# Loading the first three x tiles and wq slices in column pieces over two DMA queues, with a shorter warm-up filler

## Chip, cores, metric

One core of one Trainium2 chip. The metric is the device time of one execution in microseconds (us), as the median of several executions. A ratio is the mean time of one kernel's fast runs over the mean of the other's in the same rounds, so it isn't quite the ratio of the medians that stand beside it; below 1 is faster. The intervals are 95% intervals.

## The reference, cut to what matters

The kernel mixes a linear-attention block and an MLP block over the same input `x` (2048 tokens, 640 columns, bf16). Only its beginning matters here: `x @ wqkv`, of which the first third gives the queries.

```python
def _A_ref(x, wqkv, wo):
    B, S, D = x.shape
    H = 32; Dh = D // H
    qkv = (lambda x, *d: x.transpose(*d))((x @ wqkv).reshape(B, S, 3, H, Dh), 2, 0, 3, 1, 4)
    q, k, v = qkv[0], qkv[1], qkv[2]
    phi = lambda t: jnp.where(t > 0, t + 1, jnp.exp(t)) + 1e-6
    ...
x = A_x
g = _sigmoid((x * gate_w).sum(-1, keepdims=True))
return g * a + (1 - g) * b      # a: attention block, b: MLP block
```

## The kernel before

`x` is held as 16 tiles of 128 tokens; `wq` (and `wk`, for the keys, which the profile calls wkg) as 5 slices of 128 rows. A whole tile or slice is 128 rows of 1280 B, 160 KB. A product of tile t and slice k needs tile t turned (columns to partitions) and slice k. The first loads are issued from two queues, SyncE ("sp") and ScalarE ("act"):

```python
load_x(0)                # all load_x on "sp"
load_wq(0, "act")
load_x(1)
load_wq(1, "act")
load_x(2)
load_wq(2, "act")
load_wq(3, "sp")
load_wq(4, "act")
load_wk(0, "sp")
...                      # wk 1 to 4, x tiles 3 and 4
x_turn(3)                # tiles from 3 on are turned by a DMA, issued from "sp"
...
for t0, t1 in ((5, 8), (8, NT)):
    dma_in(x_tok[:, t0:t1, :], ...)                  # 480 KB, then 1280 KB
    for t in range(4 if t0 == 5 else t0, t1):
        x_turn(t)
```

TensorE first runs fillers on a constant (to raise its clock and to pass the time), then turns tiles 0 to 2 itself (five 128-column transposes each, copied out of PSUM by VectorE) and takes up the products as slices arrive. A pair (t, k) is a matmul of 512 columns and one of 128; (t, None) is the turn of tile t.

```python
WARM = 3456              # six fillers of 512 columns, three of 128
addA(("warm",), 0.0, lambda: warmup(WARM, 0.834))
addA(("tx", 0), 0.28, lambda: t_x(0))
addA(("warm", 1), 0.0, lambda: warmup(WARM2, 0.42))
addA(("q", 2), 4.08, q_three)
def q_three():
    order = [(0, 0), (1, None), (0, 1), (1, 0), (1, 1), (2, None), (0, 2), (1, 2), (2, 0), (2, 1), (2, 2),
             (0, 3), (0, 4), (1, 3), (1, 4), (2, 3), (2, 4)]
    stream(order, wq, 128, lambda t, b: phi(b, pq_tok[:, t + 1, :]))
```

## Time and profile before

| | before |
|---|---|
| median of six runs | 260.03 us (259.23 to 260.79) |
| profiled execution, span | 257.8 us |
| TensorE busy | 98% |
| x tile 0 complete (issued 0.79) | 3.85 us |
| wq slice 1, slice 2 complete | 4.85, 6.46 us |
| first product with slice 1, with slice 2 (start of its weight load) | 5.05, 6.50 us |

"Complete" is the time at which the last of the 16 DMA engines that carry a transfer has reported. The prediction below shows the views themselves. The span is counted from the first instruction, so it is about 1.2 us shorter than the time of the execution.

### The profile page before, as it was taken

What the parts mean: (1) busy time and instruction counts of PE and PEld (TensorE: products, weight loads), DVE (VectorE), ACT (ScalarE), POOL (GpSimd) and SP (SyncE); (2) the same over time, 40 slices, a digit from 0 to 9 for tenths busy, and PEclk for the clock granted to TensorE, in tenths of its full rate; (3) what the DMA queues carried; (4) which work ended last, traced back from release to release, by engine and by line L of the source; (5) the groups of instructions that cost most, each with busy time, mean ns of one, the idle gap of its engine ahead of it and who ended that gap; (6) DMA issues with size and microseconds to landing.
All of it is one profiled execution on the core that took longest, in us unless ns stands there. A gap on an engine that the chain in (4) does not pass through costs nothing.

```text
span 257.8 us, 3932 instructions
## 1 busy us (share of the span) xinstructions
PE 253.0 (98%) x1485; PEld 126.4 (49%) x1512; DVE 144.2 (56%) x286; ACT 108.2 (42%) x221; POOL 90.4 (35%) x144
## 2 busy tenths in 40 slices
PE   8999999999999999999999999999999999999996
PEld 4555555544454544555444445444444744445554
DVE  2697888899964993679999600499600033200023
ACT  1497676651366858675853321001540100253000
POOL 5011499976952162658917000133100021300000
DMA  7766699646636699474646620114200022200011
GB/s 220 208 152 212 118 149 220 190 93 121 124 79 80 123 397 293 85 80 76 127 45 123 123 51 3 31 25 127 53 0 0 3 59 73 102 4 0 0 51 53
DMA packets 55891, 26.25 MB, mean 102 GB/s; under 512 B 47252, under 2 KB 54461, under 8 KB 55872
## 3 DMA queue, kind: packets, MB, share of 16 engines
q1 hardware_dynamic: 53696, 21.61, 38.5%
q0 software_dynamic: 1168, 3.28, 5.3%
q10 hardware_dynamic: 1008, 1.11, 1.2%
q8 instruction: 12, 0.20, 0.3%
q14 instruction: 7, 0.06, 0.1%
HBM read 12.04 MB, written 2.62 MB: 57 GB/s over the span
## 4 chain that ended last, share of the span: by engine, by line
PE 95%; DMA 2%; ACT 1%; issue 1%; DVE 0%; ACTq 0%
PE ps L604 51%; PE ps L1218 30%; PE ps L808 8%; DMA wq<-in_A_wqkv_dram 2%; PE ps L925 2%; PE ps L1253 1%; ACT hsT L660 1%; PE ps L1131 1%; PE ps L926 1%; DVE x_tok L643 0%; PE ps L1012 0%; PE ps L1041 0%; ACTq L285 0%; ACT junk L659 0%
## 5 line engine op out<-in xcount | busy, mean ns | idle before, releaser
L604 PE MATMUL ps<-xnT,w 128*128 128x512 bf16 x350 | 80.0, 379 | 0.5 <-issue 0.2
L643 DVE SCALAR_TENSOR_TENSOR x_tok<-ps,stg,abx 128x512 bf16<-128x512 f32 (+1 forms) x20 | 13.3, 670 | 80.6 <-PE ps L1218 58.6
L660 ACT ACTIVATE h2T<-ps 128x512 bf16<-128x512 f32 x52 | 30.5, 598 | 61.6 <-PE ps L604 61.5
L604 PEld LDWEIGHTS ps<-xnT,w 128*128 128x128 bf16 x360 | 34.5, 98 | 39.7 <-issue 0.5
L1218 PE MATMUL ps<-w,h2T 128*128 128x512 bf16 (+1 forms) x254 | 47.7, 346 | 0.3
L626 POOL TENSOR_SCALAR xn<-x_tok,st 128x640 bf16<-128x640 bf16 x32 | 35.2, 1107 | 25.7 <-DMA xnT<-xn 25.2
L626 POOL TENSOR_SCALAR abx<-x_tok,stg 128x640 f32<-128x640 bf16 x16 | 15.4, 970 | 70.8 <-DVE x_tok L643 70.8
L1218 PEld LDWEIGHTS ps<-w,h2T 128*128 128x128 bf16 x260 | 23.2, 98 | 24.5 <-issue 0.3
L660 ACT ACTIVATE Er<-ps 128x640 bf16<-128x640 f32 (+1 forms) x35 | 22.9, 660 | 14.9 <-PE ps L604 10.1
L659 ACT ACTIVATE junk<-x_tok 128x640 bf16<-128x640 bf16 x32 | 23.6, 737 | 2.8 <-DVE x_tok L641 2.5
L660 ACT ACTIVATE hsT<-ps 128x512 bf16<-128x512 f32 (+1 forms) x32 | 19.0, 594 | 11.3 <-PE ps L604 10.8
L604 PE MATMUL ps<-w,hsT 128*128 128x128 bf16 (+1 forms) x159 | 23.5, 298 | 0.2
L604 PE MATMUL ps<-wkg,xT 128*128 128x512 bf16 (+1 forms) x138 | 21.3, 298 | 0.1
L641 DVE SCALAR_TENSOR_TENSOR x_tok<-ps,x_tok 128x640 bf16<-128x640 f32 x16 | 13.1, 820 | 12.2 <-ACT junk L659 7.7
L1218 PE MATMUL ps<-M_sb,pqnT 128*128 128x512 bf16 (+1 forms) x98 | 19.6, 347 | 0.1
L604 PEld LDWEIGHTS ps<-w,hsT 128*128 128x128 bf16 x160 | 13.3, 98 | 12.3
L1160 DVE TENSOR_TENSOR pq_tok<-pq_tok,dnr 128x300 bf16<-128x300 bf16 (+1 forms) x48 | 18.5, 438 | 0.6
L808 PE MATMUL ps<-pk_tok,x_tok 128*128 128x512 bf16 x78 | 17.6, 379 | 0.1
L604 PEld LDWEIGHTS ps<-wkg,xT 128*128 128x128 bf16 x140 | 11.9, 97 | 11.2
L626 DVE TENSOR_SCALAR Er<-Er 128x640 bf16<-128x640 bf16 (+1 forms) x35 | 12.2, 348 | 8.0 <-ACT Er L660 7.4
L634 DVE TENSOR_TENSOR qprod<-qprod,pk_tok 128x640 f32<-128x640 f32 x13 | 16.3, 1252 | 0.4
L604 PE MATMUL ps<-wq,xT 128*128 128x512 bf16 (+1 forms) x69 | 16.2, 367 | 0.1
(89 smaller groups left out, 234.5 us busy)
## 6 DMA issues: line engine op xcount, KB each, us to landing
w<-in_B_w_dram SPq DMA_DIRECT2D x1, 2160.0 KB, 9.9
w<-in_B_w_dram SPq DMA_DIRECT2D x1, 2080.0 KB, 15.5
out_dram<-x_tok SPq DMA_DIRECT2D x3, 640.0 KB, 3.2
x_tok<-in_A_x_dram SPq DMA_DIRECT2D x1, 1280.0 KB, 6.4
w<-in_B_w_dram POOLq DMA_DIRECT2D x8, 160.0 KB, 4.6
x_tok<-in_A_x_dram SPq DMA_DIRECT2D x5, 160.0 KB, 3.9
wv<-in_A_wqkv_dram POOLq DMA_DIRECT2D x1, 800.0 KB, 5.6
wq<-in_A_wqkv_dram ACTq DMA_DIRECT2D x4, 160.0 KB, 4.2
```

Source lines behind the costliest of these rows:

```text
L604: ins = e.matmul(out_ap, l, r, start=(i == 0), stop=(i == n - 1))
L626: return engf(lambda e: e.tensor_scalar(out_ap, in_ap, s1, s2, op0, op1), rd, [out_ap], cost=cost)
L634: return engf(lambda e: e.tensor_tensor(out_ap, a, b_, op), [a, b_], [out_ap], cost=cost)
L641: return dve(lambda e: e.scalar_tensor_tensor(out_ap, in0, scalar, in1, op0, op1, accum_out=accum), rd, [out_ap, accum], cost=cost + 70.0)
L643: return dve(lambda e: e.scalar_tensor_tensor(out_ap, in0, scalar, in1, op0, op1), rd, [out_ap], cost=cost)
L659: return act(lambda e: e.activation(out_ap, in_ap, func, bias=bias, scale=scale, accum_out=accum), rd, wr, cost=cost)
L660: return act(lambda e: e.activation(out_ap, in_ap, func, bias=bias, scale=scale), rd, wr, cost=cost)
L808: ins = e.matmul(o, l, r, start=(t0 + q_ == 0), stop=(t0 + q_ == NT - 1))
L925: e.matmul(ps[:, b, 0:512], l, w[:, k, 0:512], start=(k == 0), stop=(k == KD - 1))
L926: return e.matmul(ps[:, b + 1, 0:n2], l, w[:, k, 512:512 + n2], start=(k == 0), stop=(k == KD - 1))
L1160: dve(lambda e, o=o, i0=i0, i1=i1: e.tensor_tensor(o, i0, i1, ALU.mult), [i0, dnr[:, 1, sd, :]], [o], cost=cost)
L1218: ins = e.matmul(o, l, r, start=first and i == 0, stop=last and i == len(prs) - 1, skip_group_check=True)
```

## The change

The intent is to have x tile 0 sooner by letting both queues carry it, and to start the real work earlier by as much: the filler loses one 512-column matmul. All six first transfers are cut, so twelve are issued.

```diff
-    load_x(0)
-    load_wq(0, "act")
-    load_x(1)
-    load_wq(1, "act")
-    load_x(2)
-    load_wq(2, "act")
+    for i in range(3):
+        for queue, n0, n1 in (("sp", 0, 256), ("act", 256, D)):
+            sch.dma(queue, x_tok[:, i, n0:n1], x2[128 * i:128 * (i + 1), n0:n1], "x%d%s" % (i, queue))
+        for queue, n0, n1 in (("sp", 256, D), ("act", 0, 256)):
+            sch.dma(queue, wq[:, i, n0:n1], A_wqkv[128 * i:128 * (i + 1), n0:n1], "wq%d" % i, group_total=2)
...
-    WARM = 3456
+    WARM = 2944
```

## The prediction

> **What bounds the kernel now.** I read the page first: engine shares, then the chain that ended last.
>
> ```profile
> PE 253.0 (98%) x1485; PEld 126.4 (49%) x1512; DVE 144.2 (56%) x286; ACT 108.2 (42%) x221; POOL 90.4 (35%) x144
> ...
> PE 95%; DMA 2%; ACT 1%; issue 1%; DVE 0%; ACTq 0%
> PE ps L604 51%; PE ps L1218 30%; PE ps L808 8%; DMA wq<-in_A_wqkv_dram 2%; PE ps L925 2%; PE ps L1253 1%; ACT hsT L660 1%; PE ps L1131 1%; PE ps L926 1%; DVE x_tok L643 0%; PE ps L1012 0%; PE ps L1041 0%; ACTq L285 0%; ACT junk L659 0%
> ```
>
> TensorE is busy 98% of the span and is 95% of the chain. The one other piece of size is the load of wq, 2% of 257.8 us or about 4.7 us: the start. Only that start is touched by the change, so I went there: the chain of waits in time order, then the waits of the first 14 us.
>
> ```profile
> 1.72 4.73 DMA wq<-in_A_wqkv_dram
> 6.50 0.39 PE ps L925
> ...
> PEld ps L615 <- DMA x_tok<-in_A_x_dram: 0.3, 1, 0.3
> PEld ps L925 <- issue: 0.3, 1, 0.3
> PEld ps L925 <- DMA wq<-in_A_wqkv_dram: 0.3, 1, 0.3
> ```
>
> The chain passes from the issue of wq slice 2 at 1.72 us through its landing to the matmul at 6.50 us. The columns of the waits are total, times, longest. So before 6.50 TensorE has three holes of 0.3 us each (until x tile 0 lands; until its turned copy is there, put down to "issue"; until wq slice 2 lands). After 6.50 no DMA wait is listed for it up to 14 us. What TensorE does in those first microseconds, from the timeline of that engine (start, duration, instruction):
>
> ```profile
> 0.83 2.93 PE L881 MATMUL ps<-const-bfloat16-1.0 128*128 128x512 bf16 x9 [0.83 <-PEq L1448]
> 3.90 0.45 PE L615 MATMUL ps<-ident,x_tok 128*128 128x128 bf16 x5
> ...
> 4.53 0.38 PE L925 MATMUL ps<-wq,xT 128*128 128x512 bf16 x1
> 4.75 0.22 PE L926 MATMUL ps<-wq,xT 128*128 128x128 bf16 x1
> 4.80 0.46 PE L615 MATMUL ps<-ident,x_tok 128*128 128x128 bf16 x5
> 5.10 0.38 PE L925 MATMUL ps<-wq,xT 128*128 128x512 bf16 x1
> ...
> 5.92 0.44 PE L615 MATMUL ps<-ident,x_tok 128*128 128x128 bf16 x5
> ...
> 6.50 0.39 PE L925 MATMUL ps<-wq,xT 128*128 128x512 bf16 x1
> ```
>
> The nine fillers (six of 512 columns, three of 128) end where x tile 0 arrives. How hard the load path works, from the table of one-microsecond stretches (the last two columns are the busy share of the 16 DMA engines and GB/s):
>
> ```profile
> 2.00:3.00 1.00, 1.00 (x4) 0.39 (x3) 0.00 (x0) 0.00 (x0) 0.92 (x6) 1.00 0.63 198
> 3.00:4.00 1.00, 0.86 (x7) 0.42 (x6) 0.00 (x0) 0.34 (x1) 0.84 (x4) 1.00 1.07 388
> 4.00:5.00 1.00, 0.87 (x12) 0.59 (x12) 0.65 (x2) 0.94 (x1) 0.72 (x5) 1.00 1.04 358
> 5.00:6.00 1.00, 1.00 (x13) 0.63 (x11) 0.71 (x3) 0.00 (x0) 0.00 (x0) 1.00 0.94 287
> 6.00:7.00 1.00, 0.86 (x12) 0.51 (x9) 0.57 (x3) 0.00 (x0) 0.00 (x0) 1.00 1.06 359
> ```
>
> From 3 us on the DMA engines are full. The start is bound by their bytes, not by when transfers are issued: wq slice 3 is issued at 2.18 and lands at 7.29, a backlog of several microseconds.
>
> **What the Trainium skill says.** "DMA: Bandwidth & Descriptors", section "Issuing engines are not separate DMA queues": transfers from different issuers run on the same 16 engines and interleave; using more issuers saves only sequencer time. The trace agrees: x tile 0 (one queue) and wq slice 0 (the other), both issued at 0.8, land at 3.85 and 4.02, so neither had the engines alone. The same page, section "Why small descriptors are slow (HBM only)", speaks of a fixed overhead per packet. The trace agrees: a packet of 256 B takes 18 ns, one of 1024 B 46 ns, one of 1280 B 55 ns, one of 3456 B 135 ns (medians of the packet records), a line of 8.7 ns plus 0.0365 ns per byte. "TensorE: Matmul & The Clock Gate", Part 1, says the array runs at half clock until a free-running window of about 3.4 us was busy. The trace agrees on the step: fillers of 512 columns start 427 ns apart, and between 3.45 and 3.54 us the 128-column ones tighten; after that pairs of 512 and 128 columns start 270 ns apart.
>
> **The change part by part.** Instruction order on TensorE, VectorE and GpSimd is unchanged except for one 512-column filler less and a split wait before the first transposes.
>
> Filler: minus 427 ns, so its last matmul starts at about 3.1 and the queue is free at about 3.2 instead of 3.6 us. Worth something only if x tile 0 is there sooner.
>
> x tile 0: both queues now carry it first. Its 64 KB on the first queue used to be the first 64 of 160 KB. From packet records binned by 0.2 us, that queue has moved 64 KB by about 2.65 and 160 KB by 3.21; the landing of the whole came 0.64 later, so the small piece lands near 3.3. The other queue starts at 2.22, has 96 KB by about 3.1, lands near 3.65. So x tile 0 is complete some 0.2 us earlier than 3.85; its first block, which alone gates the first matmul, 0.5 earlier.
>
> First matmul: it now waits for wq slice 0, in both queues behind the x pieces, near 4.15 (4.02 before plus packet overhead). Against 4.50 that is a gain of 0.3 us, at this point.
>
> Packet overhead: a row of 1280 B is 55 ns of an engine; 512 plus 768 B is 27.4 + 36.7 = 64.1 ns (estimates from the line above). Each engine moves 8 rows of each 160 KB transfer: 8 x 9 = 73 ns more, and 9 ns for one more semaphore write: 0.08 us per transfer, on engines that are full. By the sixth transfer that is 0.08 x 6 = 0.49 us, of which about 0.1 lies in the slow first stretch, where the engines wait anyway.
>
> wq slice 2: each queue carries the same 480 KB up to it as before, so it lands at 6.46 + 0.4 = 6.85 us if its slowest engine sets it as before, or about 6.5 if spreading evens that out (x tile 2 landed at 5.58, so the other queue was ahead). This is the **last wait of the start**, and it decides: after it TensorE runs without holes. The 0.3 gained at the first matmul is eaten at slices 1 and 2: I get 5.2 for the second slice's matmul (5.05 before) and 6.5 to 6.85 for the third's (6.50 before).
>
> Issue: 12 issues instead of 6, each about 0.45 us, 6 per queue: the last piece of slice 2 is issued at 3.15 us, not 1.72. Supply is 160 KB per 0.47 us, demand 160 KB per 0.53 us (8 x 64.1 + 18 ns), so issue stays just ahead of the engines. ScalarE's table load moves from 3.66 to about 5.1 and ends near 6.4, before the first exponential at 8.61: free.
>
> Later loads come 0.5 us later: wq slice 3 lands at 7.8 and wk slice 2 at 10.1 where the stream took them up at 7.87 and 10.05; with the stream itself 0.15 later that just fits, and costs 0.1 at most if it doesn't. The turned x tiles have over 0.7 us to spare (tile 4 lands at 15.49, is used at 16.3).
>
> Sum: the matmul stream after 6.5 us starts between 0.0 and 0.35 us later, 0.15 in the middle; against 260.07 that is plus 0.1%.
>
> **The rivals.**
> First, the intended gain: if the slow early packets (up to 0.67 us, before 2.4 us) overlap better over two queues, and the even split removes the slow tail of slice 2, the third wait shrinks: minus 0.3 us or a little more, 259.7. For: the three holes are 0.9 us together. Against: engines at 1.04 to 1.07 busy from 3 us.
> Second, the clock: with less filler and new holes from 3.2 on, the busy window may be missed and the next one ends some 3.4 us later. The first four pairs (270 ns more each) and the fifteen transposes (56 ns more each) then run at half speed: 1.9 us, less some 0.6 us of holes that they fill, so 1.3, 261.4. For: the old step came at 3.5, close to the cut. Against: about 2.4 of the first 3.5 us stay busy.
> Third, issue becomes the bound: pieces of 64 KB every 0.45 us leave the engines idle; slice 2 would land after 7, plus 0.5 us or more, 260.6.
>
> **Range and chances.** All paths lie within 0.6% of the time before, and its own three runs span 259.23 to 260.79, which is wider than the effect. I take plus 0.15, 260.2 us, and plus or minus 1.0 for the spread of runs and the clock: 259.2 to 261.2. Two per cent is 5.2 us, more than the whole start could give or take: chances 0.01 faster, 0.98 within, 0.01 slower.
>
> **What would show it.** Right: transposes of x tile 0 start before 3.7, the first matmul on wq near 4.2, the third slice's first matmul at 6.5 to 6.85 still released by the load of wq, and DMA packets up by some 860 (128 more rows and 16 more semaphore writes in each of six transfers). Rival one: that matmul at 6.2 or earlier. Rival two: 512-column matmuls 427 ns apart past 4 us. Rival three: DMA share clearly below 1 between 3 and 6 us. I am wrong if the time moves by over 1 us, or if a wait appears after 7 us that was not there.

## The result

The changed kernel takes 261.06 us (six runs, 260.5 to 261.72) against 260.03: ratio 1.004, interval 1.0015 to 1.0065. That is within 2%, but it is a real loss of about 1.0 us.

The page of the changed kernel: engine shares, the packet count, and the chain that ended last.

```profile
PE 255.4 (98%) x1511; PEld 126.6 (49%) x1511; DVE 144.5 (56%) x286; ACT 108.3 (42%) x221; POOL 90.0 (35%) x144
...
DMA packets 56755, 26.26 MB, mean 101 GB/s; under 512 B 47348, under 2 KB 55325, under 8 KB 56736
...
PE 92%; DMA 5%; SPq 2%; DVE 0%; issue 0%
```

The chain's DMA share went from 2 to 5%, and the issuing queue of SyncE, not there before, has 2%. Packets are up by 864. TensorE's timeline of the start (L615 is the turn, L924 the 512-column part of a product, L925 in the kernel before):

```profile
3.24 0.74 PE L615 MATMUL ps<-ident,x_tok 128*128 128x128 bf16 x5
...
4.12 0.45 PE L924 MATMUL ps<-wq,xT 128*128 128x512 bf16 x1
...
4.82 0.62 PE L615 MATMUL ps<-ident,x_tok 128*128 128x128 bf16 x5 [0.18 <-DMA x_tok<-in_A_x_dram]
6.06 0.39 PE L924 MATMUL ps<-wq,xT 128*128 128x512 bf16 x1 [0.62 <-DMA wq<-in_A_wqkv_dram]
...
7.03 0.44 PE L615 MATMUL ps<-ident,x_tok 128*128 128x128 bf16 x5
...
7.62 0.39 PE L924 MATMUL ps<-wq,xT 128*128 128x512 bf16 x1
```

The first turn comes 0.66 us earlier (3.90 before) and the first product 0.41 earlier (4.53). Then the gain is lost: the second turn is level (4.80), slice 1's first product 0.96 us later (5.10), slice 2's 1.12 later (6.50). The waits of the first 30 us, those of TensorE's weight load (total us, times, longest; L604 are the later products):

```profile
PEld ps L924 <- DMA wq<-in_A_wqkv_dram: 1.4, 3, 0.8
PEld ps L604 <- DMA xT<-x_tok: 1.1, 1, 1.1
PEld ps L615 <- DMA x_tok<-in_A_x_dram: 0.9, 2, 0.6
PEld ps L924 <- DMA wkg<-in_A_wqkv_dram: 0.5, 1, 0.5
```

Waits for wq grew from 0.3 to 1.4 us, those for x from 0.3 to 0.9, and two are new: for wk slice 2 (at 11.4 us) and for turned tile 4 (at 18.8). And the table of one-microsecond stretches (last two columns: share of the DMA engines, GB/s), to be held against the one in the prediction:

```profile
3.00:4.00 1.00, 1.00 (x10) 0.79 (x8) 0.23 (x1) 0.00 (x0) 0.84 (x4) 1.00 0.88 235
4.00:5.00 1.00, 0.77 (x4) 0.23 (x3) 0.42 (x1) 0.00 (x0) 0.71 (x5) 1.00 0.85 230
5.00:6.00 1.00, 0.44 (x5) 0.23 (x4) 0.71 (x3) 0.90 (x1) 0.00 (x0) 1.00 0.97 264
6.00:7.00 1.00, 0.94 (x6) 0.42 (x6) 0.00 (x0) 0.38 (x1) 0.00 (x0) 1.00 0.90 284
```

The loads moved at 230 to 284 GB/s, not 287 to 388, and the engines were no longer full. What completed when (last engine's report, us):

| | before | changed, first trace | changed, second trace |
|---|---|---|---|
| x tile 0 | 3.85 | 3.25 | 3.26 |
| wq slice 0 | 4.02 | 4.08 | 3.85 |
| x tile 1 | 4.64 | 5.00 | 5.02 |
| wq slice 1 | 4.85 | 6.01 | 5.57 |
| x tile 2 | 5.58 | 6.90 | 6.42 |
| wq slice 2 | 6.46 | 7.57 | 7.21 |

The two traces first compared differ by 2.5 us in span (260.3 against 257.8), more than the medians, because the one of before is of a short execution (259.03 us, below all six timed ones) and the one of the changed kernel of one of its longer ones (261.54). So I trust the medians for the size and the traces for the place. By the starts of the weight loads, TensorE's loss in that trace grows in four steps: 1.0 us at slice 1, 1.1 at slice 2, 1.45 at wk slice 2 (11.45 against 9.99), 2.56 at turned tile 4 (18.84 against 16.28). After that it stays.

### The profile page after: what moved, and what is told of

It is laid out like the page before. It is cut to its first block, busy times and chain, and to the rows that moved or that the text cites. A ratio compares the mean times of both kernels' runs of the same rounds, so it can differ in the third digit from the quotient of the medians.

```text
span 260.3 us, 3966 instructions
## 1 busy us (share of the span) xinstructions
PE 255.4 (98%) x1511; PEld 126.6 (49%) x1511; DVE 144.5 (56%) x286; ACT 108.3 (42%) x221; POOL 90.0 (35%) x144
## 3 DMA queue, kind: packets, MB, share of 16 engines
q10 hardware_dynamic: 1440, 1.11, 1.3%
## 4 chain that ended last, share of the span: by engine, by line
PE 92%; DMA 5%; SPq 2%; DVE 0%; issue 0%
PE ps L604 51%; PE ps L1217 30%; PE ps L807 8%; DMA x_tok<-in_A_x_dram 2%; DMA xT<-x_tok 2%; SPq L285 2%; PE ps L1252 1%; PE ps L1130 1%; SPq L281 0%; DVE x_tok L643 0%; PE ps L1011 0%; PE ps L1040 0%
## 5 line engine op out<-in xcount | busy, mean ns | idle before, releaser
L604 PE MATMUL ps<-xnT,w 128*128 128x512 bf16 x360 | 81.3, 379 | 0.0
L604 PEld LDWEIGHTS ps<-xnT,w 128*128 128x128 bf16 x360 | 34.6, 98 | 39.7 <-issue 0.5
L1217 PE MATMUL ps<-w,h2T 128*128 128x512 bf16 (+1 forms) x260 | 48.3, 347 | 0.0
L604 PE MATMUL ps<-w,hsT 128*128 128x512 bf16 (+1 forms) x160 | 23.7, 299 | 0.0
L604 PE MATMUL ps<-wkg,xT 128*128 128x130 bf16 (+1 forms) x140 | 21.4, 299 | 0.0
L604 PEld LDWEIGHTS ps<-w,hsT 128*128 128x128 bf16 x160 | 13.3, 98 | 12.3
L604 PE MATMUL ps<-wq,xT 128*128 128x512 bf16 (+1 forms) x70 | 16.4, 368 | 0.9 <-DMA xT<-x_tok 0.9
L604 PEld LDWEIGHTS ps<-wkg,xT 128*128 128x128 bf16 x140 | 11.9, 97 | 11.2
```

The costliest lines, as they stand in the source:

```text
L604: ins = e.matmul(out_ap, l, r, start=(i == 0), stop=(i == n - 1))
L1217: ins = e.matmul(o, l, r, start=first and i == 0, stop=last and i == len(prs) - 1, skip_group_check=True)
```

## The experiments

Twelve kernels ran in three groups; each group shared its runs of the kernel before (medians 259.6, 259.79 and 259.83 us, eleven runs each). All results were correct. Theories: A1, the smaller rows slow the DMA engines; A2, the number of transfers (and of their issues) does; B, the shorter filler does; C, part is TensorE's clock.

### The changed kernel once more (after_again)

> The changed kernel once more, for the spread of its start between executions. If what its first trace shows is the rule (wq slice 1 complete at 6.0 us, DMA rate 230 to 285 GB/s from 3 to 8 us, TensorE 1.1 us on hold for turned x tile 4), those numbers come back within 0.3 us and the ratio is 1.004. If that trace was an unlucky one, slice 1 lands near 5.1 and tile 4 is in time; the trace's total is then about 1 us shorter.

Measured: 260.61 us, ratio 1.005 (1.0025 to 1.0074). Its trace (third column above) has wq slice 1 at 5.57 and 213 to 262 GB/s from 3 to 6 us, but no wait for tile 4. So late loads are the rule; the wait for tile 4 comes in some executions only.

### Split without the shorter filler (split_only), filler without the split (filler_only)

```diff
 # split_only: the changed kernel with
-    WARM = 2944
+    WARM = 3456
```

> Column pieces as in the changed kernel, filler of 3456 columns as before. Theory A (the pieces slow the loads): the loss stays, ratio 1.003 to 1.005, since TensorE waits for wq slice 1 either way. Rival B (the shorter filler lets the clock rise later and that is the loss): ratio 1.000.

```diff
 # filler_only: the kernel before with
-    WARM = 3456
+    WARM = 2944
```

> Loads as before, filler 512 columns shorter. Theory A: TensorE idles 0.4 us longer for x tile 0 and nothing after it moves, ratio 1.000 within 0.002. Rival B: the clock rises later, the first matmuls are 427 ns apart past 4 us, ratio 1.003 or more.

Measured: split_only 260.75 us, 1.0039 (1.0016 to 1.0062); filler_only 259.8, 1.0009 (0.9985 to 1.0034). The loss is the split's; rival B falls as the main cause. filler_only's trace shows how much one execution can vary with the loads of before: 14 of the 16 engines had delivered wq slice 2 by 6.46 us, the last at 7.88. In the trace of before, 15 had by 5.74 and the last at 6.46. Its clock also rose only at 5.85 us (judged by matmul spacing), not 3.45.

### The same twelve transfers with whole rows (rows_split)

```diff
+        for queue, p0, p1 in (("sp", 0, 64), ("act", 64, 128)):
+            sch.dma(queue, x_tok[p0:p1, i, :], x2[128 * i + p0:128 * i + p1, :], "x%d%s" % (i, queue))
+        for queue, p0, p1 in (("sp", 64, 128), ("act", 0, 64)):
+            sch.dma(queue, wq[p0:p1, i, :], A_wqkv[128 * i + p0:128 * i + p1, 0:D], "wq%d" % i, group_total=2)
```

> The same twelve transfers over the same queues, but each tile cut between partitions 63 and 64: rows stay 1280 B, so the packets of before (55 ns) and no more of them. Theory A1 (it is the overhead of the smaller packets, 64 against 55 ns a row): the loss goes, DMA rate back above 350 GB/s from 3 us, ratio 0.998 to 1.001. Rival A2 (it is the twelve issues at 0.47 us each, with 80 KB each, that leave DMA engines without work): DMA share below 0.95 from 3 to 6 us, ratio 1.003 to 1.006 as in the changed kernel.

Measured: 261.42 us, 1.007 (1.0043 to 1.0097). Stretches from 3 to 6 us:

```profile
3.00:4.00 1.00, 0.88 (x9) 0.61 (x8) 0.11 (x1) 0.00 (x0) 0.84 (x4) 1.00 0.75 201
4.00:5.00 1.00, 0.47 (x5) 0.21 (x4) 0.54 (x2) 0.00 (x0) 0.71 (x5) 1.00 0.82 246
5.00:6.00 1.00, 1.00 (x7) 0.61 (x7) 0.23 (x1) 0.00 (x0) 0.00 (x0) 1.00 0.85 237
```

With rows of 1280 B and packets of 55 ns (median) the loss is there all the same, so A1 can't be its main cause. That it is larger isn't shown: the interval overlaps that of after_again. But this kernel issues more slowly: an issue of half the partitions mostly took about 0.6 us, against 0.43 to 0.45 for all 128.

### Six whole loads and six tiny ones (issue_only)

```diff
     for i in range(3):
         load_x(i)
+        sch.dma("sp", junk[0:16, 0, 64 * i:64 * i + 64], x2[0:16, 0:64], "idle%d" % i)
         load_wq(i, "act")
+        sch.dma("act", junk[0:16, 0, 192 + 64 * i:256 + 64 * i], x2[0:16, 0:64], "idle%d" % (3 + i))
```

> The six whole-tile loads of before, filler of 3456, with a tiny transfer (16 rows of 128 B into an unused strip) issued after each of the six, so that the k-th whole load is issued where the changed kernel issues its k-th pair of pieces. Theory A2 (late issue, two issues for each 160 KB): wq slice 2 is issued near 2.6 us instead of 1.72, DMA share falls below 0.95 between 3 and 6 us, and much of the loss comes, ratio 1.002 to 1.005. Theory A1 (smaller rows): packets stay at 55 ns, ratio 0.999 to 1.001.

Measured: 261.62 us, 1.0051 (1.0023 to 1.008): the whole loss, with whole rows, the old filler, and 2 KB more per tiny transfer. Slice 2 was issued at 2.68 and complete at 7.01 (1.72 and 6.46 before). A2 called it.

```profile
3.00:4.00 1.00, 0.99 (x7) 0.45 (x6) 0.00 (x0) 0.00 (x0) 0.82 (x4) 1.00 0.90 245
4.00:5.00 1.00, 0.82 (x8) 0.35 (x6) 0.65 (x2) 0.00 (x0) 0.73 (x5) 1.00 0.88 261
5.00:6.00 1.00, 0.54 (x7) 0.39 (x7) 0.27 (x2) 0.93 (x1) 0.00 (x0) 1.00 0.96 292
```

Share and rate are nearer to the changed kernel's than to those of before (mean 266 GB/s from 3 to 6 us, against 243 and 344). What TensorE waited for from 3 us on was x tiles above all:

```profile
PEld ps L615 <- DMA x_tok<-in_A_x_dram: 1.6, 3, 0.8
```

This trace also tells loads and clock apart. It is of the shortest of six executions (260.12 us), and its clock was up by 3.9 us: the turns of tile 0 come 56 ns apart. Still its span is 1.1 us longer than that of before (258.9 against 257.8), and it is 0.9 us behind at the third turn (6.83 against 5.92). So late loads alone can cost about 1 us. Four of its six executions took 261.6 to 261.98; what these had on top, no trace shows.

### Small rows in six issues (pairs_small)

```diff
-    load_x(1)
-    load_wq(1, "act")
-    load_x(2)
-    load_wq(2, "act")
+    for n0, n1 in ((0, 256), (256, D)):
+        sch.dma("sp", x_tok[:, 1:3, n0:n1], x2[128:384, n0:n1].rearrange("(k p) d -> p k d", p=128), "x12", group_total=2)
+        sch.dma("act", wq[:, 1:3, n0:n1], A_wqkv[128:384, n0:n1].rearrange("(k p) d -> p k d", p=128), "wq12", group_total=2)
```

> The reverse: still six issues before wq slice 3, but tiles 1 and 2 of x and slices 1 and 2 of wq come together, cut in columns 256 and 384, so four of six transfers have the small rows in 256 KB and 192 KB at an issue. Tile 1 completes only with tile 2, which costs time of its own, so the rate is what counts. A1: DMA rate from 3 to 6 us falls from 344 (mean of 388, 358, 287) to about 300 GB/s by the packet times alone, at a share of 1. A2: issue is well ahead, share stays above 0.98. If the rate falls to 250 or less as in the changed kernel, small rows are the main cause after all.

```profile
3.00:4.00 1.00, 1.00 (x8) 0.52 (x7) 0.00 (x0) 0.24 (x1) 0.82 (x4) 1.00 1.11 344
4.00:5.00 1.00, 1.00 (x8) 0.49 (x6) 0.65 (x2) 1.00 (x1) 0.74 (x5) 1.00 1.08 308
5.00:6.00 1.00, 0.19 (x2) 0.00 (x0) 0.00 (x0) 0.04 (x1) 0.00 (x0) 1.00 0.95 293
```

Mean 315 GB/s (344 + 308 + 293, over 3) at a share of 0.95 to 1.11. The small rows cost some 8% of the rate (344 before), as their packet times say (27 and 36 ns measured, 27.4 and 36.7 predicted). They don't empty the engines. The time, 262.08 (1.0069, 1.0034 to 1.0104), says nothing on rows: tile 1 was complete only with tile 2, at 6.45 us.

### Fewer pieces (x0_cols, first_pair)

```diff
 # x0_cols: only tile 0 is cut; then load_wq(0, "act"), load_x(1), load_wq(1, "act") ... whole
+    for queue, n0, n1 in (("sp", 0, 256), ("act", 256, D)):
+        sch.dma(queue, x_tok[:, 0, n0:n1], x2[0:128, n0:n1], "x0%s" % queue)
 # first_pair: the changed loop for i in range(1), the rest whole
```

> Only x tile 0 comes in two column pieces over both queues; wq slice 0 follows whole, tiles 1 and 2 as before; short filler. It keeps the part of the change that worked (x tile 0 at 3.25 instead of 3.85 us). A1 and A2 both leave only one more transfer, so the loss should mostly go: ratio 0.998 to 1.001, first matmul on wq near 4.1, slice 2 complete within 0.3 us of the kernels with whole loads. If the loss stays at 1.003, the cause is x tile 0's own split or the order it forces on wq slice 0.

> The step between: x tile 0 and wq slice 0 in pieces (two issues more than before), the rest whole, short filler. Theory A2 (each added issue of 0.47 us sets back all that follows on both queues): between x0_cols (1.000, half an issue on each queue more) and the changed kernel (1.005, three more): 1.001 to 1.002, slice 2 issued at 2.2 instead of 3.15 us. If splitting as such were harmful, not the number of issues, it would be near 1.004.

Measured: x0_cols 259.6 us, 0.9998 (0.9972 to 1.0025); first_pair 259.83, 1.0009 (0.9974 to 1.0045). With one, two and six transfers more than before the ratio is 1.000, 1.001 and 1.004 to 1.007; the intervals of the first two are too wide to tell them apart. x0_cols has tile 0 at 3.21 us and 332 and 373 GB/s from 3 to 5, but slice 1 at 5.57: the weight load for its first product with slice 1 starts at 5.61, 0.56 later than before, with slice 2 at 6.72, 0.22 later (slice 2 itself was there at 6.31). In its trace the earlier tile 0 buys nothing, since slice 1 sets the pace. By the ratios it beats the changed kernel, not the one before.

### Turning tile 4 before the big load (after_turn4)

```diff
     x_turn(3)
+    x_turn(4)
...
-        for t in range(4 if t0 == 5 else t0, t1):
+        for t in range(t0, t1):
```

> The changed kernel with the turn of x tile 4 issued before the 480 KB load of tiles 5 to 7 instead of behind it. If the wait for tile 4 near 18 us (1.1 us in the changed kernel's trace, none in its second trace) is a real part of the loss, the ratio falls from 1.005 to 1.002 or 1.003 and no wait for a turned tile shows before 20 us. If only the first 8 us matter, it stays at 1.004 to 1.005; if the later tiles now miss their time, a wait appears at tile 5 or 8 and it gets worse.

Measured: 262.25 us, 1.0083 (1.0053 to 1.0114), worse, though in its trace nothing waits for a turned tile any more. The whole loss of that trace is in the first 10.2 us, which the edit hardly touches, and its timeline shows what it is:

```profile
8.22 0.59 PE L925 MATMUL ps<-wq,xT 128*128 128x512 bf16 x1
8.60 0.31 PE L926 MATMUL ps<-wq,xT 128*128 128x128 bf16 x1
8.71 0.63 PE L925 MATMUL ps<-wq,xT 128*128 128x512 bf16 x1
...
10.21 0.38 PE L925 MATMUL ps<-wq,xT 128*128 128x512 bf16 x1
10.42 0.22 PE L926 MATMUL ps<-wq,xT 128*128 128x128 bf16 x1
10.48 0.38 PE L925 MATMUL ps<-wq,xT 128*128 128x512 bf16 x1
```

From 8.60 to 8.71 a 128-column matmul holds the array 107 ns, and a pair takes 0.53 us; from 10.21 on a pair takes 0.27. So the clock was at half until about 10 us here, with no hole to hide it: the four pairs from 8.22 to 10.21 alone cost some 0.9 us (1.99 us, against 4 x 0.27). In the two traces of the changed kernel itself the spacing tightened at about 4.3 and 6.0 us, in rows_split at 9.3, in pairs_small at 9.7. That the edit itself made it worse isn't shown; its interval overlaps that of after_again, and one trace can't say how often the clock is late.

### Fillers in the holes (after_filled, before_filled, x0_filled)

```diff
-        order = [(0, 0), (1, None), (0, 1), (1, 0), (1, 1), (2, None), (0, 2), ...
+        order = [(0, 0), (None, None), (1, None), (None, None), (None, None), (0, 1), (1, 0), (1, 1), (None, None), (2, None), (None, None), (0, 2), ...
```

A (None, None) is two fillers of 128 columns.

> The changed kernel with ten more fillers of 128 columns put into the holes in front of x tile 1 (2), wq slice 1 (4), x tile 2 (2) and wq slice 2 (2). Theory C (part of the loss is the clock: the holes of late loads let its release be missed in some executions, 4.3 us in one trace, 6.0 in the next, 9.8 in another kernel with these loads): no execution is near 262, the spread narrows, ratio 1.002 to 1.003. If only the late loads count, the clock costs nothing on the median and the ratio stays at 1.004 to 1.005, or 1.006 where a filler stands in the way.

> The control: the same ten fillers in the kernel before. They cost at most 10 times 56 ns when warm, 0.56 us, less the 0.26 us that was a hole. Theory C: its unlucky executions (260.5 to 261.2) go, and the ratio is 0.998 to 1.001. Without C: 1.001 to 1.002.

> Only x tile 0 split, short filler, with the ten fillers in the holes: the candidate to beat both. Theory C: every execution near 259.3, ratio 0.997 to 0.999. Without C: like x0_cols, 1.000 to 1.001.

Measured: after_filled 260.87 us, 1.0046 (1.0014 to 1.0077), with executions up to 262.25; before_filled 260.68, 1.0024 (0.9997 to 1.0051); x0_filled 260.15, 1.0007 (0.9981 to 1.0033). The test failed by its own making, as a wait in before_filled between 4 and 8 us shows:

```profile
PEld ps L881 <- DVE xT L669: 0.6, 2, 0.4
```

The fillers write a PSUM bank that VectorE was still copying a turned tile out of, so they waited and held up slice 1's first product: 6.18 us instead of 5.05, though slice 1 was there at 4.74. x0_filled had the narrowest spread (259.75 to 260.46) but no better time. How much of the changed kernel's 1 us is the clock stays open; that the loads suffice for it, issue_only's trace shows.

## Why the prediction was right or wrong

The time lay in the range, and the class was right; the plus of 0.15 us was not. It was about 1.0. That the time fell inside was the width of the range, and in part luck: the upper end, 261.2, was 0.14 us away. Both of the prediction's own signs of being wrong came: the median moved by 1.03 us, and waits appeared after 7 us. By its steps:

- **Filler and x tile 0: right in direction, too small.** The two pieces were complete at 3.01 and 3.25 us, not 3.3 and 3.65. First turn 3.24, first product 4.12 ("near 4.15").
- **Packet overhead: right, and not the point.** 864 packets more, 27 and 36 ns. pairs_small shows its worth alone: 8% of the rate at a full share.
- **Issue, and engines that stay full: this step failed.** "Supply is 160 KB per 0.47 us, demand 160 KB per 0.53 us (8 x 64.1 + 18 ns), so issue stays just ahead of the engines." The 0.47 us is right (1.25, 1.71, 2.18 ... 3.13), and in sum issue did stay ahead: the last of the twelve pieces (960 KB) was issued at 3.17 to 3.62 us, and at 5.00 only 718 KB had been moved (finished packets of the first trace; the very first packet came 1.0 us after its issue). What failed is the other half, "engines that are full". The twelve transfers of 80 KB on average moved at 230 to 264 GB/s between 3 and 6 us, well under the supply of about 349 (163,840 B in 0.47 us), with engines at 0.85 to 0.97. issue_only, with whole rows, and rows_split, with halves by partitions, show low rates too. Why the engines fall below what is issued, the traces don't tell, nor whether single engines ran out of work while others had some (packets carry no engine number): issue_only shows that the added transfers are enough, not which part of handling them costs it.
- **wq slice 2, and the sum: wrong in size through that.** The third wait did decide more than the first gain, as said, but slice 2 came at 7.57 and 7.21, not 6.5 to 6.85; slice 1's product at 6.05 and 5.61, not 5.2.
- **Later loads and turned tiles: wrong.** The prediction had "just fits, and costs 0.1 at most if it doesn't". But wk slice 2 was waited for in both traces (0.5 us in each), turned tile 4 in one (1.1 us). The spare 0.7 us was less than the delay of the queue ahead of it: x tile 4 was complete at 12.24 us, not 10.39.
- **The rivals.** The first happened up to the first product, then was paid back. The third, issue as the bound, named the right signs (share below 1 from 3 to 6 us, slice 2 after 7) and was sized at "plus 0.5 us or more"; that the engines lacked issued work isn't shown (718 of 960 KB, above). The second, the clock, was seen at about 10 us in a kernel with the changed loads and costs some 0.9 us there; in the two traces of the changed kernel it rose at 4.3 and 6.0, largely under waits.

## What to carry to other kernels

Where loads set the start, count the transfers ahead of the one that decides, and compare their rate with what whole tiles reach: here six tiny transfers of 2 KB cost as much as cutting six tiles in twelve. Getting the first operand sooner bought nothing here, as a later one set the pace. Before filling holes of TensorE, check that the fillers' PSUM bank is free, and take several traces of a start: the slowest of 16 engines and the clock move it by a microsecond between executions.

## What the Trainium skill lacked or had wrong

- "DMA: Bandwidth & Descriptors", section "Issuing engines are not separate DMA queues": it calls the time to initiate a DMA usually small relative to the DMA. Here an issue took 0.43 to 0.45 us, and the 160 KB that it starts 8 x 55 = 440 ns on each engine, so the two are about equal, and for pieces issue isn't small; six added transfers of 2 KB, with their issues, cost 0.5% (issue_only).
- The same page, section "Rules for kernel authors", advises against two transfers to disjoint partition halves, since they share the engines. The runs agree (rows_split, 1.007) and add what it lacks: issuing half the partitions mostly took longer (about 0.6 us) than issuing all of them (0.43 to 0.45).
- "TensorE: Matmul & The Clock Gate", Part 1, has the release after a free-running window of 3.4 us, varying by half a microsecond from run to run. That is for sustained work; with the holes of these starts the traces show 3.45 to about 10 us. The granted clock, as the profile gives it, reads 1.00 in every trace that was kept (the page warns that clock events can be unreliable), so here only the spacing of matmuls tells. Three executions without a trace read 0.993; they took 262.08 to 262.43 us.
- No page has a figure for the spread of the 16 engines over one transfer: for wq slice 2 it was 1.1 us in the trace of before (5.36 to 6.46) and 2.8 us in that of filler_only (5.07 to 7.88), with the same loads.
